# Retention and a two-layer MLP on one core: q loaded by the parity of the head, rows put in place by the stores

## The chip, the core and the metric

The kernel runs on one core of a Trainium2 chip. The metric is the device time of one launch in microseconds (us). The core has a matrix engine (TensorE, PE in the profile), VectorE (DVE), ScalarE (ACT), GpSimd (POOL) and SyncE (SP), and 16 DMA engines that move data between HBM and the on-chip memory. Transfers are issued from the queues of SP, ACT and POOL.

## The reference

Eight batches, eight heads, 576 positions, head size 64; then an MLP over the 4608 tokens with 512 inputs, 2048 hidden values and 512 outputs.

```python
scores = scale * np.matmul(q, k.transpose(0, 1, 3, 2))      # q, k, v: (8, 8, 576, 64), float32
Dmat = np.where(rel >= 0, gamma[:, None, None] ** rel[None, :, :], 0.0)   # rel = query - key
attn_out = np.matmul(scores * Dmat[None], v)                # (8, 8, 576, 64)
x = attn_out.transpose(0, 2, 1, 3).reshape(B * S, H * D)    # 4608 tokens x 512
h = x @ w_in
out = (h * np.cos(h)) @ w_out                               # 4608 x 512, float32
```

Each head has its own decay gamma. The decay by distance is split into a factor on q (growing with the position in a chunk) and one on v (falling), so that a chunk needs a mask of zeros and ones only, and a running state carries what lies before it.

## The kernel before, in words

**Chunks.** A batch is cut into five chunks r of up to 128 positions: four of 128 and one of 64. `ns_of(r)` is 2 or 1, the number of consecutive tokens that one partition holds of a chunk. Partitions 0 to 63 hold heads 0 to 3 and partitions 64 to 127 heads 4 to 7.

**Loads (`load`, lines 273 to 283).** q, k and v of a chunk are each loaded by two transfers on SP's queue, one for each half of the heads. A transfer runs over 64 partitions, 4 heads and one run of `ns` tokens of 64 floats: 256 runs of 512 B (256 B in the short chunk). The staging tiles kn, qn and vn exist once per chunk index r, so the load of the next batch waits for the casts of this one.

**Preparation (`prep_dma`, lines 326 to 336).** POOL casts k to bf16 (`kcast`), multiplies q and v by their decay factors (`decay`, line 317, with the tables UQ and WV), and one DMA transpose on SP (line 332) puts k and q with the head's 64 dimensions on partitions into KQT, which exists twice (batch even or odd). Then SP issues the loads of a chunk that lies three chunks further on. SP's queue is in order: transpose of one chunk, then six loads of a later one. Batches 0 and 1 are transposed on PE instead (`turn`, line 338, copied out by ACT in line 348).

**Attention.** `scores` (line 372) multiplies k and q of a chunk on PE into the two banks SC; DVE multiplies by the mask MK into RT (line 389). `rest` (line 394) adds the part from the running state (ps from kqt and sb), the part within the chunk (ps from rt and vb) and the new state. ACT copies the result into XT (line 439), the input of the MLP in bf16, 512 channels over 128 partitions by 4, with 1536 token columns used in a ring. That copy writes with a step of `ns`, which puts the columns into the order of the tokens. `state` (lines 444 to 459) updates the state with DVE and ACT.

**MLP.** A block j is 512 columns of XT. `mlp1` multiplies by w_in, ACT takes the cosine as a sine with an offset (line 482, tile cb) and DVE multiplies (line 485, tile gt or ss). `layer2` multiplies by w_out in seven products of half size in place of eight, with sums made by DVE; DVE totals (line 571) the result into OSB. `store` (line 490) writes 128 rows of 512 floats to HBM from ACT's queue in one transfer of 128 runs of 2 KB.

**Order of the work.** It is written out by hand in `emit` (lines 678 to 819). In the steady part, each block j runs 16 times `mlp1`, then `layer2(j)`, and between its products the five visits of batch j+1: `rest` of the chunk before and `scores` of the next one. The casts and transposes of later chunks (PREP1, PREP2) are placed in the same order. The stores of a block stand at the end of `layer2` (two, line 616) and after the fourth `mlp1` of the next block (two, line 804). The last block has an order of its own (`last_layer2`, line 621): three stores from ACT's queue (lines 647 to 650) and two from SP's (lines 660 and 662).

**Constants (`consts`, line 227).** POOL writes position numbers IP and MI with iota, DVE corrects them for the upper half of the partitions (line 243), and ACT makes UQ and WV with 16 Exp, one for each head and table (line 260).

Of the kernel before, what the change touches and what calls it, by code (L numbers as in the profile page):

```python
# [13 lines left out]
DM = H_ * D_  # L14
# [29 lines left out]
def ns_of(r):  # L44

    return ck_of(r) // 64


class Tok:
# [91 lines left out]
class _Kernel:  # L141
    def __init__(self, nc, es, q, k, v, w_in, w_out, out):
# [51 lines left out]
        self.OSB = sb("osb", [128, 4 * DM], F32)  # L194
        self.bOSB = [Buf() for _ in range(4)]
        self.IP = sb("ip", [128, NIP], F32)
        self.WV = sb("wv", [128, NIP * 4], F32)
        self.UQ = sb("uq", [128, NIP * 4], F32)
        self.MK = sb("mk", [128, 2 * CH], BF16)
# [6 lines left out]
        self.bIP, self.bWV, self.bUQ, self.bMK, self.bC, self.bID, self.bIDLE = (Buf() for _ in range(7))  # L206

        def ps(name):
            return nc.alloc_psum_tensor(name, [128, 512], F32)
# [17 lines left out]
    def consts(self):  # L227
        s = self.s
        s.op("dve", lambda e: e.memset(self.C_LN8.ap(), float(math.log(1.0 / 8.0))), writes=[Buf()])
        s.op("dve", lambda e: e.memset(self.C_PIH.ap(), float(math.pi / 2.0)), writes=[self.bC])  # L230
        s.op("dve", lambda e: e.memset(self.IDLE.ap(), 0.0), writes=[self.bIDLE])
        self.touch(AF.Exp)

        for t, b, o, n, pat, base, mul in (
                (self.IP, self.bIP, 0, NIP, [[CH, NCH - 1], [1, 2]], 0, 2),
                (self.IP, self.bIP, NIP - 1, NIP, [[0, 1]], CH * (NCH - 1), 1),
                (self.MI, self.bMK, 0, 2 * CH, [[-1, 2], [1, 2], [2, 64]], 0, -2)):
            shape = [[n, 128]] + [[1, 1]] if o else [[n, 128], [1, n - 1]] if n == NIP else [[n, 128], [128, 2], [64, 2], [1, 64]]
            s.op("pool", lambda e: e.iota(bass.AP(t, o, shape), pat, base=base, channel_multiplier=mul,
                                          allow_small_or_imprecise_dtypes=True), writes=[b])  # L240
        for o, n in ((0, NIP - 1), (NIP - 1, 1)):
            up = bass.AP(self.IP, 64 * NIP + o, [[NIP, 64], [1, n]])
            s.op("dve", lambda e: e.tensor_scalar(up, up, -128.0 if n > 1 else -64.0, None, ALU.add),
                 reads=[self.bIP], writes=[self.bIP])
# [12 lines left out]
        for t, b, sign in ((self.UQ, self.bUQ, 1.0), (self.WV, self.bWV, -1.0)):  # L257
            for h in range(H_):
                hs, hh = divmod(h, 4)
                s.op("act", lambda e: e.activation(  # L260
                    bass.AP(t, 64 * hs * 4 * NIP + hh, [[4 * NIP, 64], [4, NIP]]),
                    bass.AP(self.IP, 64 * hs * NIP, [[NIP, 64], [1, NIP]]), AF.Exp, scale=sign * self.lng[h],
                    **(dict(bias=bass.AP(self.C_LN8, 64 * hs, [[1, 64], [1, 1]])) if sign > 0 else {})),
                    reads=[self.bIP, self.bC], writes=[Buf()])
            b.w = [Tok("act", "act", s.count["act"], {})]

    def touch(self, f):

# [16 lines left out]
    def w_in_load(self, i, after=()):  # L285
        n = DFF // NWI
# [22 lines left out]
        self.s.op(eng, fn, reads=[self.bST32["k"][r]], writes=[self.bKB[i][r]])  # L309

    def decay(self, eng, x, b, r):
        ns, i = ns_of(r), b % 2
        if x == "q":
            o, bt, w, bw = self.by_head(self.KQ[i][r], 256 * ns, 512 * ns, ns, D_, 256), self.bQB[i][r], self.UQ, self.bUQ
        else:
            o, bt, w, bw = self.by_head(self.VB[i][r], 0, 256 * ns, ns, D_ * ns, D_), self.bVB[i][r], self.WV, self.bWV
        self.s.op(eng, lambda e: e.tensor_tensor(  # L317
            o, self.by_head(self.ST32[x][r], 0, 256 * ns, ns, D_ * ns, D_),
            bass.AP(w, r * 8, [[4 * NIP, 128], [1, 4], [4, ns], [0, D_]]), ALU.mult),
            reads=[self.bST32[x][r], bw], writes=[bt])  # L320

    def kqt(self, i, r, x, n):

# [48 lines left out]
    def scores(self, b, r):  # L372
        s, ns, i = self.s, ns_of(r), b % 2
        W, nq = 2 * NP * S_, 64 * ns
        mms = []
        for c in range(2):
            for sl in range(ns):
                for hs in range(2):
                    for hp in range(2):
                        k0 = 64 * hp * W + 1024 * r + c * 128 + 64 * hs  # L380
                        mms.append((
                            bass.AP(self.SC[hp], 64 * hs * 512 + (c * ns + sl) * nq, [[512, 64], [1, nq]]),
                            bass.AP(self.KQT[i], k0 + sl * 256, [[W, 64], [1, 64]]),
                            bass.AP(self.KQT[i], k0 + 256 * ns, [[W, 64], [256, ns], [1, 64]]),
                            dict(start=c == 0 and sl == 0, stop=c == 1 and sl == ns - 1, skip_group_check=True)))
        self.group(mms, [self.bKT[i][r], self.bQT[i][r]], self.bSC)
        for hp in range(2):
            p3 = [[512, 128], [ns * nq, 2], [1, ns * nq]]
            s.op("dve", lambda e: e.tensor_tensor(  # L389
                bass.AP(self.RT[r % 2][hp], 0, p3), bass.AP(self.SC[hp], 0, p3),  # L390
                bass.AP(self.MK, 0, [[2 * CH, 128], [0, 2], [1, ns * nq]]), ALU.mult),
                reads=[self.bSC[hp], self.bMK], writes=[self.bRT[r % 2][hp]])

    def rest(self, b, r, state=True):
# [3 lines left out]
        if r:  # L398
            sb = self.SB[(r - 1) % 2]
            mms += [(bass.AP(self.PS, 512 * hs + 256 * c, [[1024, 128], [1, nq]]),  # L400
                     bass.AP(sb, (2 * hs + c) * 128, [[512, 128], [1, 128]]),
                     bass.AP(self.KQT[i], 1024 * r + 256 * ns + c * 128 + 64 * hs, [[W, 128], [256, ns], [1, 64]]),
                     dict(start=c == 0, stop=False, skip_group_check=True)) for c in range(2) for hs in range(2)]
        for c in range(2):
            for sl in range(ns):
# [29 lines left out]
        for x0, po0, n in ((t0, 0, n0), (0, n0 // ns, ck - n0)):  # L435
            if n:
                o = bass.AP(self.XT, x0, [[NP * XR, 128], [XR, NP], [1, ns], [ns, n // ns]])
                p = bass.AP(self.PS, po0, [[1024, 128], [256, NP], [64, ns], [1, n // ns]])
                s.op("act", lambda e: e.activation(o, p, AF.Copy),  # L439
                     reads=[self.bPS], writes=self.bXT[x0 // GR:(x0 + n) // GR])  # L440
        if state:
# [45 lines left out]
            bass.AP(m, 0, [[512, 128], [n, k], [1, n]]), bass.AP(cb, 0, [[TB, 128], [n, k], [1, n]]), ALU.mult),  # L487
            reads=[bm, bcb], writes=[x for d in dts for x in self.g(j, d)[1]])

    def store(self, j, m, eng="act"):  # L490
        row0 = TB * j + 128 * m
        self.s.dma(eng, f"o{m}", lambda e: e.dma_start(
            bass.AP(self.out, row0 * DM, [[DM, 128], [1, DM]]),
            bass.AP(self.OSB, m * DM, [[4 * DM, 128], [1, DM]])), reads=[self.bOSB[m]])

    def half_store(self, j, m, h, eng, b):
        row0 = TB * j + 128 * m
        self.s.dma(eng, f"o{m}{h}", lambda e: e.dma_start(
            bass.AP(self.out, row0 * DM + 256 * h, [[DM, 128], [1, 256]]),
            bass.AP(self.OSB, m * DM + 256 * h, [[4 * DM, 128], [1, 256]])), reads=[b])  # L500

    def mlp2(self, j, st, part):

# [344 lines left out]
```

## Time and profile before

| what | value |
|---|---|
| median of 3 runs | 308.84 us (305.84 to 311.0) |
| the profiled execution | 309.18 us, its span 307.1 us |
| mean granted PE clock | 0.989 |
| packets of the DMA queues | 103480, 49.60 MB |
| period of one block in the steady part | 30.4 us (stores at 159.26 and 189.66) |
| median landing of a store, a q load, a transpose | 3.4, 3.4, 4.3 us after the issue |

The span runs from the first to the last instruction of the profiled execution. The page lists the busy time of each engine, the packets of each DMA queue with the share of 16 engines' time that they took, the chain of work that ended last, groups of equal instructions, and the DMA issues with the time from issue to landing. A share above 1 of the DMA engines means that the times of packets in flight overlap.

### The profile page before, as it was taken

How to read it: one execution, taken by the hardware profiler on the slowest of the kernel's cores; microseconds unless marked ns; L12 is line 12 of the kernel's file. 1: busy time of each engine (PE TensorE's matmuls, PEld its weight loads, DVE VectorE, ACT ScalarE, POOL GpSimd, SP SyncE). 2: the span in 40 equal slices, each digit the busy share in tenths (PEclk: the TensorE clock that was granted, in tenths of full speed). 3: DMA queues.
4: the chain of work that ended last, by engine and by line, in shares of the span. 5: the costliest groups of instructions: out<-in, count | busy, mean ns of one | idle time of the engine just before them, and what ended most of it. 6: DMA issues, size and time to landing. Idle time of an engine off the chain costs nothing.

```text
span 307.1 us, 8716 instructions
## 1 busy us (share of the span) xinstructions
PE 292.3 (95%) x3520; PEld 190.6 (62%) x3520; DVE 232.3 (76%) x393; ACT 190.1 (62%) x336; POOL 115.8 (38%) x133
## 2 busy tenths in 40 slices
PE   8768997999899999999999999999999999999996
PEld 3347644553587458746874687457845874685485
DVE  3347654867986898789878986999689768937963
ACT  6647845587565766576657665865576657724730
POOL 2346271999835444533551445436341000000000
PEclk9969999999999999999999999999999999999999
DMA  4999999567986987697879799977795012003003
GB/s 137 204 203 218 215 235 235 156 162 198 235 177 184 280 129 189 169 269 161 164 180 260 160 174 170 290 168 173 191 254 97 2 50 89 2 0 130 10 0 140
DMA packets 103480, 49.60 MB, mean 162 GB/s; under 512 B 45456, under 2 KB 98960, under 8 KB 103440
## 3 DMA queue, kind: packets, MB, share of 16 engines
q1 hardware_dynamic: 94176, 35.80, 54.2%
q10 hardware_dynamic: 5040, 9.05, 8.8%
q0 software_dynamic: 4224, 4.19, 8.4%
q8 instruction: 28, 0.46, 0.6%
q14 instruction: 12, 0.10, 0.1%
HBM read 36.70 MB, written 9.44 MB: 150 GB/s over the span
## 4 chain that ended last, share of the span: by engine, by line
PE 82%; DVE 5%; ACT 4%; SPq 4%; DMA 2%; issue 1%; POOL 0%; DVEq 0%; ACTq 0%
PE mm L362 59%; PE mm L364 14%; PE ps L362 6%; SPq L281 4%; PE sc L362 3%; DMA kn<-in_k_dram 2%; ACT cb L482 2%; DVE gt L485 1%; DVE ss L542 1%; DVE rt L389 1%; ACT sb L456 1%; ACT xt L439 1%; ACT kqt L348 1%; DVE ss L485 1%; DVE s L453 0%
## 5 line engine op out<-in xcount | busy, mean ns | idle before, releaser
L362 PE MATMUL mm<-xt,win 128*128 128x512 bf16 (+5 forms) x517 | 119.0, 349 | 2.0 <-DVE gt L485 1.2
L482 ACT ACTIVATE cb<-mm,c_pih 128x512 bf16<-128x512 f32 (+3 forms) x147 | 98.7, 680 | 33.7 <-PE mm L364 30.0
L485 DVE TENSOR_TENSOR gt<-mm,cb 128x512 bf16<-128x512 f32 (+1 forms) x130 | 85.7, 678 | 11.8 <-ACT cb L482 8.2
L362 PEld LDWEIGHTS mm<-xt,win 128*128 128x128 bf16 x517 | 46.8, 99 | 49.5 <-ACT cb L482 4.0
L364 PE MATMUL mm<-xt,win 128*128 128x512 bf16 (+5 forms) x147 | 54.0, 368 | 0.0
L389 DVE TENSOR_TENSOR rt<-sc,mk 128x512 bf16<-128x512 f32 (+1 forms) x80 | 44.8, 601 | 11.4 <-PE sc L364 11.4
L308 POOL CAST kq<-kn 128x512 bf16<-128x512 f32 (+1 forms) x40 | 25.2, 629 | 66.3 <-DMA kn<-in_k_dram 66.3
L317 POOL TENSOR_TENSOR kq<-qn,uq 128x512 bf16<-128x512 f32 (+1 forms) x37 | 36.9, 997 | 20.8 <-DMA qn<-in_q_dram 19.1
L362 PE MATMUL mm<-tt,ss 128*128 128x256 bf16 x336 | 43.2, 273 | 0.0
L439 ACT ACTIVATE xt<-ps 128x512 bf16<-128x512 f32 (+1 forms) x41 | 27.0, 661 | 24.6 <-PE ps L364 18.6
L317 POOL TENSOR_TENSOR vb<-vn,wv 128x512 bf16<-128x512 f32 (+1 forms) x34 | 34.4, 1013 | 17.1 <-DMA vn<-in_v_dram 14.4
L456 ACT ACTIVATE sb<-s 64x256 bf16<-64x256 f32 x64 | 26.6, 416 | 13.3 <-DVE s L453 12.1
L362 PEld LDWEIGHTS mm<-tt,ss 128*128 128x128 bf16 x336 | 31.4, 98 | 4.8
L566 ACT ACTIVATE sn<-mm 128x512 f32<-128x512 f32 x31 | 18.5, 598 | 25.1 <-PE mm L364 24.8
L542 DVE TENSOR_TENSOR ss<-gt 128x512 bf16<-128x512 bf16 (+1 forms) x56 | 32.1, 573 | 0.9
L571 DVE TENSOR_TENSOR osb<-mm,sn 128x512 f32<-128x512 f32 x30 | 20.6, 687 | 11.6 <-PE mm L364 11.3
L362 PE MATMUL mm<-wout,gt 128*128 128x256 bf16 x217 | 28.0, 273 | 0.3 <-DVE gt L485 0.3
L362 PE MATMUL mm<-wout,ss 128*128 128x256 bf16 (+1 forms) x160 | 27.4, 305 | 0.0
L453 DVE TENSOR_TENSOR s<-ps,s 128x256 f32<-128x256 f32 x24 | 10.2, 424 | 21.3 <-ACT xt L439 19.7
L364 PEld LDWEIGHTS mm<-xt,win 128*128 128x128 bf16 x147 | 14.4, 98 | 15.9
L362 PEld LDWEIGHTS mm<-wout,gt 128*128 128x128 bf16 x217 | 20.1, 98 | 4.1 <-DVE gt L485 0.5
L362 PEld LDWEIGHTS mm<-wout,ss 128*128 128x128 bf16 x160 | 15.1, 98 | 5.2
(76 smaller groups left out, 324.6 us busy)
## 6 DMA issues: line engine op xcount, KB each, us to landing
out_dram<-osb ACTq DMA_DIRECT2D x34, 256.0 KB, 3.4
kn<-in_k_dram SPq DMA_DIRECT2D x64, 128.0 KB, 3.4
qn<-in_q_dram SPq DMA_DIRECT2D x64, 128.0 KB, 3.4
vn<-in_v_dram SPq DMA_DIRECT2D x64, 128.0 KB, 3.7
win<-in_moe_w_in_dram POOLq DMA_DIRECT2D x4, 512.0 KB, 7.4
wout<-in_moe_w_out_dram POOLq DMA_DIRECT2D x4, 512.0 KB, 11.6
kn<-in_k_dram SPq DMA_DIRECT2D x16, 64.0 KB, 3.7
qn<-in_q_dram SPq DMA_DIRECT2D x16, 64.0 KB, 3.0
```

Of the source, the lines that this page charges most:

```text
L308: fn = (lambda e: e.activation(o, x, AF.Copy)) if eng == "act" else (lambda e: e.tensor_copy(o, x))
L317: self.s.op(eng, lambda e: e.tensor_tensor(o, self.by_head(self.ST32[x][r], 0, 256 * ns, ns, D_ * ns, D_), bass.AP(w, r * 8, [[4 * NIP, 12 ...
L362: self.nc.tensor.matmul(o, a, b, **kw)
L364: return s.done("pe", self.nc.tensor.matmul(o, a, b, **kw), reads, writes)
L389: s.op("dve", lambda e: e.tensor_tensor(bass.AP(self.RT[r % 2][hp], 0, p3), bass.AP(self.SC[hp], 0, p3), bass.AP(self.MK, 0, [[2 * CH, 128 ...
L439: s.op("act", lambda e: e.activation(o, p, AF.Copy), reads=[self.bPS], writes=self.bXT[x0 // GR:(x0 + n) // GR])
L456: s.op("act", lambda e: e.activation(bass.AP(self.SB[r % 2], 64 * hp * 512 + 64 * hp, [[512, 64], [128, NP], [1, D_]]), bass.AP(self.S32, ...
L482: s.op("act", lambda e: e.activation(ci, mi, AF.Sin, bias=self.C_PIH.ap(), scale=1.0), reads=[bm, self.bC], writes=[bcb])
L485: s.op("dve", lambda e: e.tensor_tensor(bass.AP(gt, dt * TB + o0, [[16 * TB, 128], [TB * step, k], [1, n]]), bass.AP(m, 0, [[512, 128], [n ...
L542: self.s.op(eng, lambda e: e.tensor_tensor(oo, xx, yy, op), reads=xb + yb, writes=ob)
L566: self.s.op("act", lambda e: e.activation(self.SN[k].ap(), bank[0].ap(), AF.Copy), reads=[bank[1]], writes=[self.bSN[k]])
L571: self.s.op("dve", lambda e: e.tensor_tensor(bass.AP(self.OSB, 2 * t * DM + 256 * h, [[4 * DM, 128], [DM, 2], [1, 256]]), bass.AP(bank[0], ...
```

## The change

- **q's load.** A chunk of q is still two transfers on SP's queue, but now one for each parity of the head. Four partition groups of 32 hold the four head pairs, and a partition holds four consecutive tokens (`nj_of`: 4, or 2 in the short chunk) of both heads of its pair. A transfer is 4 head pairs x 32 runs of 1 KB (512 B in the short chunk). k and v are loaded as before.
- **Constants.** q's factors need position numbers of their own (IQ) and, since each group of partitions has other heads, a table LG of the logarithms, written by 16 memsets. UQ takes two Exp over all partitions and WV four.
- **Scores.** The moving operand reads q's columns in runs of 32 in place of 64. The columns of a chunk are now in the queries' order of the new layout (j, then t, for token 4t + j); MI, and so the mask, follows it.
- **x.** The copy into XT no longer steps: x stays in that order, and so do the rows of the MLP's result.
- **Stores.** The token that a row belongs to is found by `rows`; a store writes 32 rows with a step of four (two) rows, once for each j. Where the 128 columns of a store lie in one chunk it is one transfer, else two of 64 rows. In two batches (nine stores) four lie in one chunk and five do not; all of the last block's do not.

```diff
     def load(self, x, b, r, after=()):
         ns = ns_of(r)
         t, bt = self.ST32[x][r], self.bST32[x][r]
+
+        def parity(h):
+            n = D_ * nj_of(r)
+            dst = bass.AP(t, h * n, [[2 * n, 128], [1, n]])
+            src = bass.AP(self.src[x], ((b * H_ + h) * S_ + CH * r) * D_, [[2 * S_ * D_, 4], [n, 32], [1, n]])
+            return lambda e: e.dma_start(dst, src)
...
-        return self.s.dma("sp", f"{x}n{r}", [half(0), half(1)], writes=[bt], after=after)
+        parts = [parity(0), parity(1)] if x == "q" else [half(0), half(1)]
+        return self.s.dma("sp", f"{x}n{r}", parts, writes=[bt], after=after)
...
+        for h in range(H_):
+            for o, n, hd in ((0, 32, 2), (2, 64, 4)):
+                p, i = h // hd, h % hd
+                s.op("dve", lambda e: e.memset(bass.AP(self.LG, n * p * 6 + o + i, [[6, n], [1, 1]]),
+                                               self.lng[h] if o == 0 else -self.lng[h]), writes=[Buf()])
...
+        for t, b, n, w, o, c in ((self.IQ, self.bIQ, 32, 2 * NIP, 0, 2 * NIP - 2), (self.IP, self.bIP, 64, NIP, 0, NIP - 1)):
+            for p in range(1, 128 // n):
+                for o, m, k in ((0, c, CH), (c, w - c, 64)):
+                    up = bass.AP(t, n * p * w + o, [[w, n], [1, m]])
+                    s.op("dve", lambda e: e.tensor_scalar(up, up, -float(k * p), None, ALU.add),
+                         reads=[b], writes=[Buf()])
...
+        for t, bt, ip, bi, o, n in ((self.UQ, self.bUQ, self.IQ, self.bIQ, 0, 2),
+                                    (self.WV, self.bWV, self.IP, self.bIP, 2, 4)):
+            for i in range(n):
...
         if x == "q":
-            o, bt, w, bw = self.by_head(self.KQ[i][r], 256 * ns, 512 * ns, ns, D_, 256), self.bQB[i][r], self.UQ, self.bUQ
+            o = bass.AP(self.KQ[i][r], 256 * ns, [[512 * ns, 128], [D_, 2], [128, nj], [1, D_]])
+            x = bass.AP(t, 0, [[256 * ns, 128], [D_ * nj, 2], [D_, nj], [1, D_]])
+            w, bw, bo = bass.AP(self.UQ, 8 * r, [[4 * NIP, 128], [1, 2], [2, nj], [0, D_]]), self.bUQ, self.bQB[i][r]
...
-                            bass.AP(self.KQT[i], k0 + 256 * ns, [[W, 64], [256, ns], [1, 64]]),
+                            bass.AP(self.KQT[i], 64 * hp * W + 1024 * r + 256 * ns + 32 * (2 * hs + c),
+                                    [[W, 64], [128, 2 * ns], [1, 32]]),
...
-                o = bass.AP(self.XT, x0, [[NP * XR, 128], [XR, NP], [1, ns], [ns, n // ns]])
-                p = bass.AP(self.PS, po0, [[1024, 128], [256, NP], [64, ns], [1, n // ns]])
+                o = bass.AP(self.XT, x0, [[NP * XR, 128], [XR, NP], [1, n]])
+                p = bass.AP(self.PS, po0, [[1024, 128], [256, NP], [1, n]])
...
-    def store(self, j, m, eng="act"):
-        row0 = TB * j + 128 * m
-        self.s.dma(eng, f"o{m}", lambda e: e.dma_start(
-            bass.AP(self.out, row0 * DM, [[DM, 128], [1, DM]]),
-            bass.AP(self.OSB, m * DM, [[4 * DM, 128], [1, DM]])), reads=[self.bOSB[m]])
+    def rows(self, c):
+
+
+        b, c = divmod(c, S_)
+        r, c = divmod(c, CH)
+        return b * S_ + CH * r + c // 32, nj_of(r)
+
+    def store(self, j, m, eng="act", h=None, b=None):
+
+        col, n = (0, DM) if h is None else (256 * h, 256)
+        (r0, s0), (r1, s1) = (self.rows(TB * j + 128 * m + 64 * i) for i in range(2))
+
+        def part(p0, row, k, step):
+            src = bass.AP(self.OSB, p0 * 4 * DM + m * DM + col, [[4 * DM, 32 * k], [1, n]])
+            dst = bass.AP(self.out, row * DM + col, [[DM, k], [step * DM, 32], [1, n]])
+            return lambda e: e.dma_start(dst, src)
+
+        fn = [part(0, r0, 4, s0)] if r1 == r0 + 2 and s0 == s1 else [part(0, r0, 2, s0), part(64, r1, 2, s1)]
+        self.s.dma(eng, f"o{m}" + ("" if h is None else str(h)), fn, reads=[b or self.bOSB[m]])
```

More of the change, by code (lines that the diff above doesn't have):

```diff
@@ L46, in ns_of, with nj_of @@
     return ck_of(r) // 64
+def nj_of(r):
+    return ck_of(r) // 32
 class Tok:
@@ L205, in __init__ @@
         self.C_PIH = sb("c_pih", [128, 1], F32)
-        self.bIP, self.bWV, self.bUQ, self.bMK, self.bC, self.bID, self.bIDLE = (Buf() for _ in range(7))
+        self.bIP, self.bIQ, self.bLG, self.bWV, self.bUQ = (Buf() for _ in range(5))
+        self.bMK, self.bC, self.bID, self.bIDLE = (Buf() for _ in range(4))
         def ps(name):
@@ L241, in consts @@
[L241 to L244, printed above, removed]
+        for t, b, o, dims, pat, base, mul in (
+                (self.IQ, self.bIQ, 0, [[2 * NIP, 128], [4, NCH - 1], [1, 4]], [[CH, NCH - 1], [1, 4]], 0, 4),
+                (self.IQ, self.bIQ, 2 * NIP - 2, [[2 * NIP, 128], [1, 2]], [[1, 2]], CH * (NCH - 1), 2),
+                (self.IP, self.bIP, 0, [[NIP, 128], [1, NIP - 1]], [[CH, NCH - 1], [1, 2]], 0, 2),
+                (self.IP, self.bIP, NIP - 1, [[NIP, 128], [1, 1]], [[0, 1]], CH * (NCH - 1), 1),
+                (self.MI, self.bMK, 0, [[2 * CH, 128], [128, 2], [32, 4], [1, 32]], [[-1, 2], [1, 4], [4, 32]], 0, -2)):
+            s.op("pool", lambda e: e.iota(bass.AP(t, o, dims), pat, base=base, channel_multiplier=mul,
+                                          allow_small_or_imprecise_dtypes=True), writes=[b])
@@ L256, in consts @@
             s.op("dve", lambda e: e.memset(self.SB[i].ap(), 0.0), writes=[self.bSB[i]])
-        for t, b, sign in ((self.UQ, self.bUQ, 1.0), (self.WV, self.bWV, -1.0)):
-            for h in range(H_):
-                hs, hh = divmod(h, 4)
+        for t, bt, ip, bi, o, n in ((self.UQ, self.bUQ, self.IQ, self.bIQ, 0, 2),
+                                    (self.WV, self.bWV, self.IP, self.bIP, 2, 4)):
+            for i in range(n):
                 s.op("act", lambda e: e.activation(
[L261 to L265, printed above, removed]
+                    bass.AP(t, i, [[4 * NIP, 128], [n, 4 * NIP // n]]), ip.ap(), AF.Exp,
+                    scale=bass.AP(self.LG, o + i, [[6, 128], [1, 1]]),
+                    **(dict(bias=self.C_LN8.ap()) if o == 0 else {})),
+                    reads=[bi, self.bLG, self.bC], writes=[Buf()])
+            bt.w = [Tok("act", "act", s.count["act"], {})]
     def touch(self, f):
@@ L311, in decay @@
     def decay(self, eng, x, b, r):
[L312 removed]
+        ns, nj, i = ns_of(r), nj_of(r), b % 2
+        t, bt = self.ST32[x][r], self.bST32[x][r]
         if x == "q":
[L314 to L320 removed]
+            o = bass.AP(self.KQ[i][r], 256 * ns, [[512 * ns, 128], [D_, 2], [128, nj], [1, D_]])
+            x = bass.AP(t, 0, [[256 * ns, 128], [D_ * nj, 2], [D_, nj], [1, D_]])
+            w, bw, bo = bass.AP(self.UQ, 8 * r, [[4 * NIP, 128], [1, 2], [2, nj], [0, D_]]), self.bUQ, self.bQB[i][r]
+        else:
+            o = self.by_head(self.VB[i][r], 0, 256 * ns, ns, D_ * ns, D_)
+            x = self.by_head(t, 0, 256 * ns, ns, D_ * ns, D_)
+            w, bw, bo = bass.AP(self.WV, 8 * r, [[4 * NIP, 128], [1, 4], [4, ns], [0, D_]]), self.bWV, self.bVB[i][r]
+        self.s.op(eng, lambda e: e.tensor_tensor(o, x, w, ALU.mult), reads=[bt, bw], writes=[bo])
     def kqt(self, i, r, x, n):
@@ L488, in mlp1 @@
             reads=[bm, bcb], writes=[x for d in dts for x in self.g(j, d)[1]])
-    def store(self, j, m, eng="act"):
-        row0 = TB * j + 128 * m
-        self.s.dma(eng, f"o{m}", lambda e: e.dma_start(
-            bass.AP(self.out, row0 * DM, [[DM, 128], [1, DM]]),
-            bass.AP(self.OSB, m * DM, [[4 * DM, 128], [1, DM]])), reads=[self.bOSB[m]])
+    def rows(self, c):
[11 more added lines that the diff above has]
+        self.s.dma(eng, f"o{m}" + ("" if h is None else str(h)), fn, reads=[b or self.bOSB[m]])
     def half_store(self, j, m, h, eng, b):
[L497 to L500, printed above, removed]
+        self.store(j, m, eng, h, b)
     def mlp2(self, j, st, part):
```

19 lines of the change are left out of this document (9 added, 10 removed).

## The prediction

> **What bounds the kernel now.** I read the busy table first, then the chain of work that ended last, then the lists of DMA queues and issues, then the windows by stage, and last single stretches of the timeline.
>
> ```profile
> span 307.1 us, 8716 instructions
> PE 292.3 (95%) x3520; PEld 190.6 (62%) x3520; DVE 232.3 (76%) x393; ACT 190.1 (62%) x336; POOL 115.8 (38%) x133
> ...
> q1 hardware_dynamic: 94176, 35.80, 54.2%
> q10 hardware_dynamic: 5040, 9.05, 8.8%
> q0 software_dynamic: 4224, 4.19, 8.4%
> ...
> PE 82%; DVE 5%; ACT 4%; SPq 4%; DMA 2%; issue 1%; POOL 0%; DVEq 0%; ACTq 0%
> ...
> out_dram<-osb ACTq DMA_DIRECT2D x34, 256.0 KB, 3.4
> ...
> qn<-in_q_dram SPq DMA_DIRECT2D x64, 128.0 KB, 3.4
> ```
>
> PE is busy for 95% of the span and holds 82% of the chain; SPq (4%) and DMA (2%) are the start alone. q1 is SP's queue (loads, transposes), q10 is ACT's (stores), q0 POOL's (weights). So shorter work elsewhere buys little, and the question is whether anything that PE waits for becomes late. The windows show what stands in reserve:
>
> ```profile
> core 0: us, PE busy (x) PEld busy (x) DVE busy (x) ACT busy (x) POOL busy (x), PEclk, DMA share, GB/s
> ...
> 159.30:189.70 30.40, 30.40 (x403) 20.60 (x401) 25.39 (x45) 20.25 (x36) 13.61 (x16) 1.00 1.02 197
> ...
> 251.50:277.50 26.00, 26.00 (x187) 17.14 (x185) 19.07 (x33) 14.50 (x23) 0.00 (x0) 1.00 0.11 41
> ```
>
> One period (a block of 512 tokens, one batch prepared) is 30.4 us, PE full throughout at granted clock 1.00. The DMA share is 1.02: packets of two queues are in flight at once, and the 16 DMA engines have little to give. Slack of the preparation: the last transposes and the use of what they make.
>
> ```profile
> 229.78 3.97 SPq L332 DMA_TRANSPOSE kqt<-kq  x3
> ...
> 249.97 0.23 PE L362 MATMUL sc<-kqt 64*64 64x64 bf16 x7
> ...
> 251.41 0.48 DVE L389 TENSOR_TENSOR rt<-sc,mk 128x128 bf16<-128x128 f32 x2
> ```
>
> The third transpose is issued at 232.5 and lands, by the shortest landing of that line (2.5 us), at 235.0; PE reads it at 250.0. So a transfer may be late by about 15 us here before PE stands.
>
> **Packet prices.** From the queue lists of windows in which one kind runs nearly alone:
>
> ```profile
> q1 hardware_dynamic: 2279, 1.10, 48.4%
> ...
> q1 hardware_dynamic: 3122, 0.77, 39.9%
> ...
> DMA  0000001999999700000000000009999997000000
> ...
> q10 hardware_dynamic: 576, 1.05, 34.9%
> ```
>
> Window 0 to 8 us, loads of 512 B: 48.4% of 16 engines times 8 us, over 2279, is 27.2 ns a packet on one engine. Window 230 to 240, transposes (250 B): 20.4 ns. Window 251 to 259, stores of 2 KB (512 of the 576): 87 ns; the DMA line of that window, the mean share of all 16 engines in slices of 0.2 us, stands at nine tenths and more during each pair of stores, so all 16 take part. A 1 KB packet, by the straight line from 27.2 to 87: 47 ns.
>
> **The change part by part.**
>
> *Start constants.* DVE gains 16 memsets at 0.06 us and eight tensor_scalars at 0.26, loses two: +2.5 us, where it stands idle 2.57 us before the first q lands. ACT drops from 16 Exp (2.8 us) to six; POOL gains two iotas of 0.19. Hidden; without that cover up to 2.5 us.
>
> *SP's issues.* A load of 256 packets holds SP 0.62 us, a transfer of 128 packets 0.34 (the half store on SP). Two q loads a chunk: 0.56 us less, 40 times, 22 us of SP's queue. On the path this counts only at the start, where the chain runs through SP until the k load of chunk 3: three chunks ahead of it, 1.7 us. Bounds 0 to -1.7, since that load then takes 7.09 us to land behind the weights.
>
> *Which engines carry q and the stores.* This decides. Before, both patterns of a load begin with 64 partitions, those of a store with 128 rows, and 16 engines share a transfer: 16 packets each of a half load, 8 of a store. The new q source begins with 4 head pairs, each of 32 rows of 1 KB; the new store's target begins with 4 (one chunk) or 2 (each of two parts). No row has a transfer with so small an outer count, so bounds: all 16 engines, or 4 and 2. The nearest rows by size say 16, but they fit a dealing by flat packet list and one by outer count equally. [...]
>
> On engine 0, per batch. k and v: eight full loads of two halves at 16 packets of 512 B, 256, and 64 of 256 B: 7.0 + 1.3 = 8.3 us. q: four full loads of two transfers at 32 packets of 1 KB, 256, and 64 of 512 B: 12.0 + 1.7 = 13.8 (was 4.1). Transposes: 4.5 times 1024 packets over 16, 288 at 20.4, 5.9. A whole store on four engines is 32 packets, 2.8 us; in two parts on two engines 64, 5.6 us (was 0.7). A batch is 4.5 blocks of 128 columns, so of nine stores in a row four stay whole and five straddle two chunks: 17.4 us per four. Sum 45.4 us against the period's 30.4 (before: 21.1). Engine 0 falls 15 us behind per period and eats the slack in one; k, v and transposes have a share on it too, so all land late. SP's queue fills, and the transposes queue behind the loads. What is late next: PE runs in order, so behind a score matmul that waits for its transpose stand the products of layer 2, and behind them ACT's sines and DVE's products; nothing else of PE can fill the gap.
>
> Sum up to the last transpose: loads 8 x 22.1 = 177; transposes 6 x 5.9 = 35; weights 256 x 47 ns = 12; stores of six blocks (12 whole, 12 split) 34 + 67 = 101. That is 325 us, begun at 2.2 (the first packets of window 0 to 8): landed at 327 instead of 235. PE then has what it had from 250.0 to 307.1: 57.1, so 384. Tail: the last five stores are all split, 3 x 5.6 + 2 x 3.0 (64 of 1 KB) = 22.8 us on engine 0, from 302.56 on plus the 1.35 us that a store takes beyond its packets, and 0.3 to the end: 327.0, i.e. 19.9 more. Span 404; the profiled execution lasted 309.18 for a span of 307.1, so 406. The median of the three runs, 308.84, is 0.3 below that one.
>
> *Parts on ACT and PE.* The copy xt now writes one run (748 ns before; 598 for the plain 128x512 copy sn): 150 ns x 31 less, of which its 1% of the chain keeps at most 0.6 us. Some 19 more issues on ACT: between nothing (0.17 each by packet count) and 0.34 each, 6.5 us, beside ACT's 30 us of waiting for PE; 0 taken. If ACT's queue fills, cb behind the store is late and gt after it. Score and ps matmuls read q in runs of 32 instead of 64: going from one run of 128 (219 ns, mm 128x128) to two of 64 (221) costs 2 ns, so four runs some 2 to 6 ns on 640, 1 to 4 us; 0 taken, since PE now waits. The q product on POOL keeps 512 elements in runs of 64: 0. The mask on DVE too.
>
> **The rivals.** *Few engines, but the two queues side by side* (an engine serves a load and a store at once). Loads and transposes are 28.0 us a period, stores 17.4, both under 30.4: no lag but the tail. ACT's three last stores are 14.2 us from 303.9 on, end 318.4: +11.3, 320.5 us. For it: a share above 1. Against: in window 128.9 to 159.3 the stores' packets take 11.9% of 16 x 30.4, 113 ns instead of 87; they wait for each other.
>
> *All 16 engines share them still* (the other side). Then q is 3.4 us per engine and batch (64 x 47 ns, 16 x 27.2) in place of 4.1, nothing is late, and only the start (-1.7 at best), xt (-0.6) and a second issue at the very end (+0.34) are left: 307 to 309.5, 308. It decides from 6.2 engines up: per period k, v and transposes are 14.2 us whatever the count, q and four stores 55 + 45 us shared by the count, and 14.2 + 100/6.2 is 30.4. For it: the stores of window 251 to 259 do keep all 16 busy. Against: their outer count was 128.
>
> **How the numbers follow.** Few engines taking turns 0.68, 406 us; its own range is 374 (10% of overlap) to 449 (stores at 113 ns, weights at the page's 98). Side by side 0.15, 320. All sixteen 0.17, 308. Range 316 to 450, which leaves out the last case and little else. A change under about 2% can't be told from none here. The last case splits into faster 0.04, same 0.12 and slower 0.01; the other two, 0.83, are slower, which makes 0.84.
>
> **What would show it.** Right: PE busy well under 95%, PE or PEld waiting for kqt's transposes; the mean DMA share falling (four engines full, twelve idle) while q and store landings grow past 5 us; SP's issues of 0.34 us stretched by full queues; a tail of some 20 us of DMA after the last DVE work. Wrong: q landing in 3 us as before and PE still at 95%. The step most in doubt is the count of engines, then whether loads and stores on one engine add up.

## The result and the profile after

The changed kernel takes 433.03 us (median of 4 runs, 430.48 to 434.32), the kernel before 308.15 us on the same chip (4 runs, 305.84 to 311.0): ratio 1.408, 95% interval 1.396 to 1.419. Forecast were 406 us and a range of 316 to 450. Ratios and intervals, here and below, are of the fast runs alone (those within 1.5% of the fastest of their kernel), medians of all runs. The profiled execution lasted 430.48 us, its span 428.6. The page of the kernel after, the lines that answer to those of before:

```profile
span 428.6 us, 8705 instructions
PE 315.0 (73%) x3520; PEld 198.4 (46%) x3520; DVE 231.0 (54%) x415; ACT 181.2 (42%) x326; POOL 114.3 (27%) x135
...
q1 hardware_dynamic: 82952, 35.80, 60.0%
q0 software_dynamic: 4224, 4.19, 6.1%
q10 hardware_dynamic: 4620, 9.04, 5.9%
...
PE 39%; DMA 27%; ACTq 11%; SPq 6%; ACT 5%; issue 3%; DVE 2%; POOL 1%; DVEq 0%; POOLq 0%
...
L391 PE MATMUL mm<-xt,win 128*128 128x512 bf16 (+5 forms) x517 | 126.8, 366 | 33.9 <-DVE gt L518 33.0
...
out_dram<-osb ACTq DMA_DIRECT2D x36, 128.0 KB
out_dram<-osb ACTq DMA_DIRECT2D x16, 256.0 KB
```

PE's share of the span falls from 95% to 73%, and in the chain from 82% to 39%; DMA (27%), ACT's issues (ACTq, 11%) and SP's (6%) take its place. The bytes are the same (queues q1, q10 and q0, in MB in the second column). The waits of the kernel after (columns: engine, line, what it waited for; us in total, times, longest) say for what:

```profile
DVE gt L518 <- ACT cb L515: 52.6, 52, 14.5
...
PE sc L391 <- DMA kqt<-kq: 37.4, 14, 12.7
PE mm L391 <- DVE gt L518: 33.0, 9, 13.8
ACT cb L515 <- issue: 31.4, 4, 15.0
```

There are two separate stalls. The scores wait 37.4 us for transposes (before, no such wait is listed); and `mm` from xt and win, the product of layer 1 on the page, waits 33.0 us for gt (DVE's product, which reads an earlier result before PE writes over it), gt for the sine cb on ACT, and cb for "issue", that is, for ACT's own queue. One of the four times, on ACT's timeline (columns: start, us, engine, line):

```profile
128.82 0.70 ACT L515 ACTIVATE cb<-mm,c_pih 128x512 bf16<-128x512 f32 x1
129.24 15.22 ACTq L538 DMA_DIRECT2D out_dram<-osb  x3
144.56 1.84 ACT L515 ACTIVATE cb<-mm,c_pih 128x512 bf16<-128x512 f32 x3 [15.04 <-issue]
```

Three store transfers hold ACT's queue for 15.22 us, and the next sine stands behind them. All 54 store issues on ACT take 73.1 us here, the longest 6.3; before, 35 took 15.3 us and the longest 1.1.

**Which engines carry a transfer.** Queue q10 counts 5040 packets before and 4620 after. The data are 35 x 128 = 4480 packets in both; the rest is 560 before, 35 transfers x 16, and 140 after, which is 16 x 4 + 38 x 2 (16 whole stores, 38 parts). So a transfer ends with one more packet on each engine that it uses (before, in the window 251 to 259 us where all 16 engines are at work, four stores count 64 packets under 512 B beside their 512 of data), and the new stores use four or two, as the prediction's sum has it. SP's queue, q1, tells the same of q: it counts 94176 - 82952 = 11224 packets less, of which 10240 are data (80 loads of 128 packets in place of 256), 960 are 80 x 12 closing packets, and 24 are those of the last stores (32 before, 8 after). The tail shows the same by its rate. The DMA list for the window 405.5 to 428.6 us of the kernel after, where only split stores are left:

```profile
DMA  0111110111111111111111111111111111111000
GB/s 25 43 43 32 50 53 18 35 35 53 50 50 50 53 53 50 50 50 57 50 50 50 50 57 50 48 50 51 50 48 50 48 48 48 48 48 50 23 20 0
```

One tenth of 16 engines and 50 GB/s: two engines of about 25 GB/s each (2 KB in 84 ns, the median of these packets, is 24.4). The parts come from ACT's queue (386 packets in this window) and from SP's (264), so both use the same two.

**Where the 121.5 us went.** The mask of chunk 4 of batches 2 and 7 cuts the span into three stages:

| kernel | start, to the mask of (2,4) | five periods, to (7,4) | one period | end | span |
|---|---|---|---|---|---|
| before | 97.6 | 153.8 | 30.8 | 55.7 | 307.1 |
| after | 122.9 | 221.2 | 44.2 | 84.5 | 428.6 |
| difference | 25.3 | 67.4 | 13.5 | 28.8 | 121.5 |

### The profile page after: what moved, and what is told of

Same layout as the page of the kernel before. It is cut to its first block, busy times and chain, and to the rows that moved or that the text cites. A ratio compares the mean times of both kernels' runs of the same rounds, so it can differ in the third digit from the quotient of the medians.

```text
span 428.6 us, 8705 instructions
## 1 busy us (share of the span) xinstructions
PE 315.0 (73%) x3520; PEld 198.4 (46%) x3520; DVE 231.0 (54%) x415; ACT 181.2 (42%) x326; POOL 114.3 (27%) x135
## 3 DMA queue, kind: packets, MB, share of 16 engines
q1 hardware_dynamic: 82952, 35.80, 60.0%
q0 software_dynamic: 4224, 4.19, 6.1%
q10 hardware_dynamic: 4620, 9.04, 5.9%
## 4 chain that ended last, share of the span: by engine, by line
PE 39%; DMA 27%; ACTq 11%; SPq 6%; ACT 5%; issue 3%; DVE 2%; POOL 1%; DVEq 0%; POOLq 0%
PE mm L391 28%; DMA kqt<-kq 21%; ACTq L538 11%; PE mm L393 6%; SPq L307 5%; DMA kn<-in_k_dram 4%; ACT cb L515 3%; PE sc L391 2%; PE ps L391 2%; DMA qn<-in_q_dram 2%; SPq L301 1%; DVE gt L518 1%; ACT sb L489 1%; POOL kq L349 0%; DVE s L486 0%
## 5 line engine op out<-in xcount | busy, mean ns | idle before, releaser
L391 PE MATMUL mm<-xt,win 128*128 128x512 bf16 (+5 forms) x517 | 126.8, 366 | 33.9 <-DVE gt L518 33.0
L515 ACT ACTIVATE cb<-mm,c_pih 128x512 bf16<-128x512 f32 (+3 forms) x147 | 95.7, 680 | 86.5 <-PE mm L393 53.4
L518 DVE TENSOR_TENSOR gt<-mm,cb 128x512 bf16<-128x512 f32 (+1 forms) x130 | 85.0, 679 | 56.2 <-ACT cb L515 52.6
L391 PEld LDWEIGHTS mm<-xt,win 128*128 128x128 bf16 x517 | 47.9, 102 | 88.5 <-DVE gt L518 40.2
L393 PE MATMUL mm<-xt,win 128*128 128x512 bf16 (+5 forms) x147 | 56.3, 383 | 0.0
L391 PE MATMUL mm<-tt,ss 128*128 128x256 bf16 x336 | 46.1, 284 | 0.0
L391 PE MATMUL sc<-kqt 64*64 64x128 bf16 (+1 forms) x536 | 16.1, 231 | 38.9 <-DMA kqt<-kq 37.4
L349 POOL TENSOR_TENSOR vb<-vn,wv 128x512 bf16<-128x512 f32 (+1 forms) x34 | 35.2, 1036 | 22.0 <-DMA vn<-in_v_dram 20.8
L472 ACT ACTIVATE xt<-ps 128x512 bf16<-128x512 f32 (+1 forms) x41 | 22.2, 544 | 31.6 <-PE ps L393 28.8
L391 PEld LDWEIGHTS mm<-tt,ss 128*128 128x128 bf16 x336 | 32.6, 101 | 6.1 <-issue 0.3
L391 PEld LDWEIGHTS sc<-kqt 64*64 64x64 bf16 x536 | 10.1, 114 | 44.5 <-DMA kqt<-kq 39.0
L391 PE MATMUL mm<-wout,gt 128*128 128x256 bf16 x217 | 30.5, 289 | 0.0
L391 PE MATMUL mm<-wout,ss 128*128 128x256 bf16 (+1 forms) x160 | 29.5, 320 | 0.0
L586 DVE TENSOR_TENSOR ss<-gt 128x512 bf16<-128x512 bf16 (+1 forms) x56 | 28.3, 506 | 0.9
```

The costliest lines, as they stand in the source:

```text
L349: self.s.op(eng, lambda e: e.tensor_tensor(o, x, w, ALU.mult), reads=[bt, bw], writes=[bo])
L391: self.nc.tensor.matmul(o, a, b, **kw)
L393: return s.done("pe", self.nc.tensor.matmul(o, a, b, **kw), reads, writes)
L472: s.op("act", lambda e: e.activation(o, p, AF.Copy), reads=[self.bPS], writes=self.bXT[x0 // GR:(x0 + n) // GR])
L515: s.op("act", lambda e: e.activation(ci, mi, AF.Sin, bias=self.C_PIH.ap(), scale=1.0), reads=[bm, self.bC], writes=[bcb])
L518: s.op("dve", lambda e: e.tensor_tensor(bass.AP(gt, dt * TB + o0, [[16 * TB, 128], [TB * step, k], [1, n]]), bass.AP(m, 0, [[512, 128], [n ...
```

## The experiments

Two theories. **Theory A**, the prediction's: engine 0 carries a share of everything, and the sum of the packets on it sets the pace (45.4 us a period). **Theory B**: the engine that issues a transfer stands still while few engines take its packets, so the price is paid on ACT, and by the transposes behind it. Layouts with all 16 engines then tell what else the change costs. All times are medians, against the kernel before on the same chip (308.55 to 309.12 us).

**The two halves apart.** The q load of the change with the stores of before; and the kernel before with the new stores alone.

```diff
  e1 (from after):   fn = [part(...)]  ->  one transfer of 128 rows
  e7 (from before):  store()           ->  the store() and rows() of the change
```

> The changed kernel, with the stores as before the change (one transfer of 128 adjacent rows, 16 engines), so that the output's rows stay in the queries' order and are not put in place; the q loads stay on four engines. Theory (packets pile up on the first engines): engine 0 has 8.3 + 13.8 + 5.9 + 2.8 = 30.8 us of packets a period against 30.4, so it just keeps up; the stalls of ACT in its stores and the tail go: 309 to 325 us. Rival (the 1 KB q loads and the runs of 32 cost, the stores do not): still above 390 us. Rival (more issues and scattered rows cost, not the engines): 305 to 312 us, the same side as the theory; the other runs tell those apart.

> The kernel before, with the changed kernel's stores alone (the same transfers to the same rows, on four or two engines); q, the order of x and all else as before, so the output's rows are not in place. Theory now: the stores by themselves set the pace of the steady part, by stalling ACT while it issues them and by holding up the transposes that share engines 0 and 1; the period of a block rises by 11 to 13 us as in the run with q by head pairs, the tail by 20: 390 to 415 us. Theory of the prediction (only the sum of packets on engine 0 counts): 12.4 + 5.9 + 17.4 = 35.7 us a period against 30.4, 5 us more in each of five periods and 20 for the tail: 345 to 365 us.

e1: 332.84 us, 1.077 [1.072, 1.082]. e7: 399.66 us, 1.296 [1.289, 1.303]. In spans +24.1 and +90.6, together 114.7 of the 121.5: the halves nearly add up, and the stores are three quarters. e1 comes out above its range, and not where it was expected: its period is 31.9 us (the sum on engine 0 gives 30.8), but its start is 18.0 us longer. There the weights' packets of 1 KB on POOL's queue share the engines; they take 98 ns each (8.4% of 16 x 307.1 us over 4224, on the page of before), where the prediction had 47. That this is the reason was not tried by itself. The page and the waits of e7:

```profile
PE 36%; DMA 22%; SPq 17%; ACTq 11%; ACT 4%; issue 2%; DVE 2%; DVEq 0%
...
ACT cb L487 <- issue: 30.3, 4, 11.3
...
PE sc L367 <- DMA kqt<-kq: 20.7, 9, 8.6
```

Both stalls come back with the stores alone. Its period is 40.9 us, while the packets on engine 0 sum to 35.7 (45.4 with 4.1 for q in place of 13.8): theory A is 5 us short.

**Only the last block, and a quarter of the bytes.** e6b gives the new stores to the last block alone, e8 writes 512 B of each row's 2 KB in e7.

```diff
+        if j < NTB - 1:                     # e6b
+            fn = [one transfer of 128 rows]
-        col, n = (0, DM) if h is None else (256 * h, 256)
+        col, n = (0, DM // 4) if h is None else (256 * h, 64)      # e8
```

> The kernel before, with the changed kernel's stores in the last block alone (five stores in ten parts on two engines; the rows of that block are not in place). Theory: 22.8 us of packets on engine 0 stand after the last computing, as the prediction's tail has it: 327 to 331 us. Rival (the tail is only a wait for things late before): 309 to 313 us.

> As the run before, but each store writes only the first quarter of its rows (runs of 512 B; the other three quarters of the output are not written): the same issues on the same engines, with 27 ns a packet in place of 84. Theory (time of the packets on engines 0 and 1): the packets of a period on engine 0 are 12.4 + 5.9 + 5.4 = 23.7 us and nothing backs up; left is the longer issue of seven pieces a period: 312 to 330 us. Rival (it is the number of pieces and how they are dealt, whatever their size): within 10 us of the run before.

e6b: 329.36 us, 1.066 [1.062, 1.070]. From the start of the last DVE operation to the end it takes 23.0 us in place of 2.5, the tail by itself. e8: 317.85 us, 1.030 [1.024, 1.035], period 31.7, and ACT's 54 issues take 33.0 us, the longest 1.2. The same number of transfers, the same scattered rows and the same two or four engines: what costs most is the time of the packets on those engines; the number and the scattering are left with at most 3%.

**q on two engines.** e1 with each q load in four transfers whose outer size is 2. SP's queue counts 82976 packets as in e1 (160 x 2 closing packets in place of 80 x 4), so each uses two engines.

```diff
-            src = bass.AP(..., [[2 * S_ * D_, 4], [n, 32], [1, n]])
+            src = bass.AP(..., [[2 * S_ * D_, 2], [n, 32], [1, n]])      # for g in range(2)
```

> The run with the changed kernel's q loads and the old stores, but q in four transfers a chunk whose sources begin with 2 (two engines) instead of two that begin with 4; rows of the output stay in the queries' order. Same bytes, same runs, the same number of issues as in the run by head pairs on 16 engines (327.0 us). Theory (loads pile up by the sum of packets on engine 0): 8.3 + 27.5 + 5.9 + 2.8 = 44.5 us a period instead of 30.8, and some 45 us more in the first three batches: 395 to 440 us. Rival (number of issues on SP): 325 to 340 us.

417.16 us (two runs), 1.350 [1.342, 1.357], period 41.3 where the sum on engine 0 gives 44.5. For loads, theory A holds to within 7%: 30.8 and 44.5 against 31.9 and 41.3.

**All 16 engines by more transfers.** A group of 32 partitions has an outer size of 32, and the closing packets then show all 16 engines: ACT's queue counts 6720 packets in e9 and in e3, 4480 of data and 140 x 16, and SP's queue 85192 in e2, 2240 more than in the kernel after (160 x 16 in place of 80 x 4). e2 loads q in four such transfers and keeps the new stores; e9 writes each store in four transfers in the kernel before; e3 does both; e10 does only q, with the old stores; e4 is e10 with a copy into XT that puts the columns in order (step of four).

```diff
+            dst = bass.AP(t, 32 * p * 2 * n, [[2 * n, 32], [n, 2], [1, n]])
+            src = bass.AP(..., [[n, 32], [S_ * D_, 2], [1, n]])                          # e2, e3, e4, e10
+        fn = [part(64 * i + 32 * a, r + a, 1, s) ... for a in range(2)]                   # e3, e9
+                o = bass.AP(self.XT, x0, [[NP * XR, 128], [XR, NP], [1, nj], [nj, n // nj]])   # e4
```

> The changed kernel, with each chunk of q loaded by four transfers, one for each head pair, whose two patterns both begin with 32 (16 engines); the same 1 KB runs into the same places. Stores stay split, on four or two engines. Theory: engine 0 has 8.3 + 3.4 + 5.9 + 17.4 = 35.0 us a period against 30.4, so it falls behind by 4.6 a period, less the slack of 15, and the tail of 20 us and ACT's waits in its stores stay: 345 to 375 us. Rival (scattered rows and more issues): no gain from the loads, 425 to 440 us.

> The kernel before, with each store in four transfers of 32 rows on 16 engines (146 issues instead of 37), rows as in the run before the last, so not in place. Theory: an issue holds ACT for 0.44 us whatever its size, 12 more a period are 5.3 us of ACT in bursts of eight, behind which the sines stand: 5 to 6 us a period and 3 at the end: 335 to 350 us. Rival (that run was slow by its q loads): 309 to 315 us.

> As the run before, and each store in four transfers of 32 rows, one for each j, whose patterns begin with 32 (16 engines): the same rows to the same places, with 4 issues for a store instead of 1 or 2 (146 in all instead of 58). Theory (engines): nothing piles up; issues of ACT cost some 0.5 us a store more, beside its waits: 305 to 318 us. Rival (issues and scattered rows): more than two and a half times the issues, so above 430 us. Rival (runs of 32 on PE, the new order of x): still far above 309, since both stay.

> q loaded by head pairs on 16 engines; the copy into XT steps by four columns and puts the tokens in order, as the kernel before the change did with a step of two; stores as before, one transfer each. Theory: no piling up and no further issue on ACT; PE is the bound again: 303 to 309 us, at best 2 us below the kernel before, by the start. Rival (runs of 32 on PE cost): 1 to 4 us above the kernel before.

> The changed kernel with q loaded by head pairs on 16 engines and the stores of before (rows of the output stay in the queries' order). The copy into XT does not step. Theory: four issues of 0.61 + 3 x 0.43 us stand in place of two of 0.62 on SP, 0.7 us a chunk; SP then needs 33 us for a batch and is the bound of the steady part instead of PE: 318 to 326 us, and the rest of the run with x in order (327.7 us) is the stepping copy. Rival (the stepping copy alone made that run slower): 305 to 310 us.

| kernel | us | ratio [95%] | period | sum of ACT's store issues, longest |
|---|---|---|---|---|
| e2 | 413.84 | 1.334 [1.324, 1.344] | 43.4 | 74.7, 6.1 |
| e9 | 353.69 | 1.149 [1.142, 1.157] | 37.0 | 75.6, 1.4 |
| e3 | 354.18 | 1.138 [1.128, 1.147] | 36.7 | 72.7, 1.5 |
| e4 | 327.72 | 1.058 [1.050, 1.065] | 33.5 | 14.3, 0.7 |
| e10 | 326.98 | 1.060 [1.055, 1.065] | 33.2 | 14.2, 0.7 |

All five come out above what was expected of them, e10 by 1 us only. e2 is the one that decides (its profiled execution lasted 417.04 us): with q on 16 engines, engine 0 has 35.0 us a period, and the period is 43.4. Its waits have both stalls still:

```profile
PE mm L391 <- DVE gt L518: 35.7, 11, 10.9
...
PE sc L391 <- DMA kqt<-kq: 30.0, 10, 9.3
```

So in the kernel after the sum on engine 0 (45.4 for a period of 44.2) is no full account; the stores alone would hold it nearly as long. e9 and e3 show that ACT's issues cost on 16 engines too: 140 issues at about 0.54 us. The page of e9, and one of its waits:

```profile
PE 53%; ACTq 16%; ACT 11%; DVE 8%; issue 5%; SPq 4%; DMA 2%; POOL 0%; DVEq 0%
...
out_dram<-osb ACTq DMA_DIRECT2D x136, 64.0 KB, 2.8
...
ACT cb L487 <- issue: 25.2, 7, 4.8
```

The stores land in 2.8 us and DMA holds 2% of the chain, but ACTq and ACT 27%. PE waits for a transpose only once there, 1.5 us, so this is the price of ACT's issues without late transposes. e10 points to the same on SP's queue. The four q transfers of a chunk take 2.2 us of it in place of 1.4 (100 to 220 us), and the scores wait again; the waits of e10:

```profile
PE sc L391 <- DMA kqt<-kq: 13.1, 7, 3.8
```

e4 against e10 gives the price of the stepping copy into XT: its mean grows from 544 to 1121 ns, and the median time by 0.7 us, which these runs can't tell from nothing (the two ratios lie in each other's intervals). e3 and e9 agree, so beside dear stores q by pairs costs nothing that shows.

**Stores from POOL's queue.** e7 with its stores issued by POOL, but for three of the last block (SP's two and the half store that names ACT), so that ACT is free of them until the end.

```diff
-    def store(self, j, m, eng="act", h=None, b=None):
+    def store(self, j, m, eng="pool", h=None, b=None):
```

> As the run with the changed kernel's stores alone on the kernel before (399.7 us), with all but the five or six issues of the last block that name their queue issued from POOL's queue instead of ACT's; rows not in place. ACT then never stands in an issue. Theory A (the packets that pile up on the first engines hold up the transposes, whoever issues): transposes still land in over 10 us at worst and the run stays above 350 us; what is gained is ACT's part, some 40 us. Theory B (what counts is ACT standing behind its full queue, the late transposes only follow): below 335 us. POOL's own issues, some 50 of 0.8 us, come on top of its 116 us of work in both.

371.61 us (median; 362.18 to 374.39, too far apart for an interval). Less than e7's 399.66, far above the 308.8 of before. Its page and its waits:

```profile
q0 software_dynamic: 18368, 13.20, 18.7%
...
POOL out_dram L510 <- DVE osb L587: 59.1, 7, 22.0
...
PE sc L367 <- DMA kqt<-kq: 35.2, 15, 8.0
```

With almost no store on ACT, cb no longer waits for issues, and the scores still wait 35.2 us for transposes. But POOL now stands 59.1 us waiting for osb, and the casts that feed the transposes stand behind it. Nor are the stores the same transfers: POOL's queue counts 18368 packets, 4224 of them the weights', so 14144 for 52 stores, where ACT's queue has 4620 for 54. From 308 to 313 us, where these stores alone are moving, they move 134 GB/s, which at 25 GB/s an engine takes more than five. So the run takes the stores off ACT and off the few engines at once. The time is on the side that was expected of theory A, but the run doesn't test it and splits nothing.

**q in two transfers on 16 engines.** The last kernel keeps the change's q load, two transfers of 128 runs of 1 KB, but puts token group t and head pair p on partition 4t + p. The outer sizes are then 128 and 32, and SP's queue counts 83936 packets, 960 more than in e1 (80 x 16 closing packets in place of 80 x 4): 16 engines. PE reads q's columns with a step of four; stores and the order of XT are those of before.

```diff
-            src = bass.AP(..., [[2 * S_ * D_, 4], [n, 32], [1, n]])
+            src = bass.AP(..., [[n, 32], [2 * S_ * D_, 4], [1, n]])
-   bass.AP(self.KQT[i], ... + 32 * (2 * hs + c), [[W, 64], [128, 2 * ns], [1, 32]])
+   bass.AP(self.KQT[i], ... + 2 * hs + c,        [[W, 64], [128, 2 * ns], [4, 32]])
```

> q in two transfers of 128 runs of 1 KB as in the changed kernel, but with the token group outermost (partition 4t + pair), so that the outer counts are 32 and 128 in place of 4; PE reads q's columns with a step of four, the copy into XT steps as in the kernel with q by pairs, and the stores are those of the kernel before. Theory (the outer count alone made the q load dear, and the four transfers of the kernel with q by pairs cost SP's queue, not the data): all 16 engines take part, SP issues two fewer long pieces a chunk, the period is 30.4 to 31.0 us, PE bound, and the time 305 to 311 us, ratio 0.99 to 1.01. Rival 1 (the layout of q itself costs, on POOL or in the copy into XT): as the kernel with q by pairs, 324 to 330 us. Rival 2 (a step of four in PE's moving reads halves their rate): 20 matmuls of 128 columns a chunk take 0.05 us longer each, 1.07 us x 36 chunks, 345 us.

325.51 us, 1.052 [1.048, 1.056]; period 32.6. The theory misses: the outer count was not all of the price. Rival 1 has the time, but not the cause; the page of this kernel:

```profile
PE 310.2 (96%) x3520; PEld 197.7 (61%) x3520; DVE 230.7 (71%) x418; ACT 206.6 (64%) x326; POOL 116.4 (36%) x136
...
PE 86%; ACT 4%; DVE 3%; SPq 3%; DMA 2%; issue 1%; POOL 0%; DVEq 0%
```

PE is full at 96% and no score waits for a transpose; the last one lands 30 us before its mask (16 before the change). PE has more to do, and PE's groups by shape show where. Before:

```profile
L362 PE MATMUL sc<-kqt 64*64 64x128 bf16 x480 | 13.0, 221 | 1.2 <-ACT kqt L348 1.2
L362 PE MATMUL ps<-kqt,sb 128*128 128x128 bf16 x96 | 9.4, 220 | 2.1 <-ACT sb L456 1.4 <-DVE rt L389 0.6
```

and in this kernel (busy us, mean ns of one):

```profile
L426 PE MATMUL sc<-kqt 64*64 64x128 bf16 x480 | 20.2, 288 | 2.2 <-ACT kqt L412 2.2
L426 PE MATMUL ps<-kqt,sb 128*128 128x128 bf16 x96 | 15.0, 290 | 2.2 <-DVE rt L456 1.8 <-DVE vb L384 0.3
```

The matmuls that read q with a step of four elements take 67 to 73 ns more for 128 columns; those that read rt without a step are as before (225). The busy time of these two groups and their four smaller ones grows by 7.2 + 5.6 + 2.3 + 1.0 + 0.4 + 0.4 = 16.9 us, which is the difference of the spans, 324.0 - 307.1 (PE's busy time as a whole grows by 17.9, its idle time falls by 1.0). That is rival 2 in kind, at less than half its size: it counted the score matmuls one after the other, while those on quarters of the array overlap (480 of 221 ns are 13.0 us of busy time).

## Why the prediction came out right, and which steps were wrong

The forecast of a large loss through few DMA engines was right; the time was 6% low. Of the two mechanisms that the runs show, it had one, the packets on few engines, and put the other, ACT standing in its issues, at nothing. That the period came out to 3% is in part luck.

- **Four and two engines: right.** No trace of the kernel before shows a count below 16, so the four and the two in the forecast's sum were the author's estimate. The closing packets (140 on ACT's queue, 960 fewer for q on SP's) and the 50 GB/s of the tail show them. Both rivals fall: 16 engines by the same count, side by side because the transposes do land late, up to 18.8 us after their issue (6.0 before).
- **Packets on engine 0 add up: right for loads, incomplete for stores.** That q's four engines and a store's two or four have one in common is an estimate too: the traces do not say which engine took a packet, and only the tail shows two queues on the same two. The period of 45.4 against 44.2 looks like proof and isn't, since e2 (35.0 against 43.4) and e7 (35.7 against 40.9) break the sum.
- **"0 taken" for more issues on ACT: the mis-sized term.** The prediction gave 19 more issues at most 6.5 us and left it at "if ACT's queue fills, cb behind the store is late". cb is late: ACT's issues take 73.1 us in place of 15.3, and even the shortest of them 0.52. How much of a store's price is ACT's and how much is the late transposes' stays open. e11 was to split it and changes both. e9 shows 41.3 us of span for 140 issues with hardly a wait for transposes, but those are other issues than these 54.
- **Transposes landing at 327: 336.0 measured.** Nine us late. The weights' packets at 98 ns in place of 47 would alone be 256 x 51 ns = 13 us, if they hold an engine that long; which term makes up for it was not tried.
- **PE's remaining 57.1 us.** From the landing to the first of the last stores the prediction had 302.56 - 250.0 = 52.6 us; it took 403.25 - 336.0 = 67.2. PE had three chunks to catch up, and is 6.7 us later at the last mask; then ACT stands in six issues for 9.0 us between 344.8 and 355.4 (one sine alone waits 6.28 us for two of them), and from that mask to the first of the last stores it is 8.0 more. This is the largest part of the 24.6 us by which the span exceeds the forecast (9.0 + 14.7 + 0.9).
- **Tail: right.** 24.45 us forecast from the first of the last stores to the end, 25.35 measured.
- **22 us of SP's queue saved: wrong.** The 0.34 us came from a store. A q load of 128 packets on 16 engines takes SP 0.61 us (e12), as one of 256 did. On four engines the 80 q issues take 73.8 us in all, against 60.3 before, since SP's issues stretch. From SP's timeline of the kernel after:

```profile
222.92 4.81 SPq L307 DMA_DIRECT2D vn<-in_v_dram  x2
227.83 8.65 SPq L361 DMA_TRANSPOSE kqt<-kq  x1
```

- **Small terms.** The copy xt fell from 661 to 544 ns in the mean. Runs of 32 on PE: the score matmuls take 224 ns in place of 221 in e10. Both were taken as nothing, rightly.
- **The signs.** PE well under 95%, waits for kqt, stretched issues and the tail all showed. That the DMA share would fall did not: it stands at 0.99 in 159 to 203 us, most likely since the time of a packet includes its waiting behind others: SP's packets of 256 B take 62.9 ns in the mean, 25.7 before, with a median of 18 in both. Only the tail, with one kind of transfer, shows the two engines. The landings of q loads and stores could not show, as the page of the kernel after gives none for them.

No version here beat the kernel before. Each way to a q load of long runs costs 5% or more: few engines (e1, 7.7%), more issues (e10, 6.0%), a step in PE's reads (e12, 5.2%).

## What to carry to other kernels

Before a transfer's patterns are changed, read their two outermost sizes: for the loads and stores from SP's and ACT's queues here, the number of DMA engines was 16 where both were 32 or more, and the smaller size where that was 4 or 2. The packets of one of them, times their price, were nearly the time where nothing else was on them (22.8 us by that sum in a tail of 25.35). Price a transfer on the queue that issues it as well, even when its landing is hidden: ACT spent 73.1 us in 54 issues here, and its sines stood 31.4 us behind them. And look for the full engine among those that read a new layout first: in e12 PE, at 96%, paid 16.9 us for it.

## What the runs showed of the hardware

**PE's granted clock behind one wait.** The windows of the kernel after, behind a wait of PE of 4.25 us that ends at 226.46:

```profile
core 0: us, PE busy (x) PEld busy (x) DVE busy (x) ACT busy (x) POOL busy (x), PEclk, DMA share, GB/s
...
226.40:231.50 5.10, 5.04 (x12) 1.79 (x13) 3.87 (x9) 2.32 (x4) 0.61 (x1) 0.50 2.41 145
232.40:235.90 3.50, 3.50 (x18) 1.61 (x17) 2.96 (x5) 2.65 (x5) 0.00 (x0) 1.00 0.13 51
```

PE is full in both, but at granted clock 0.50 in the first, for 5.1 us, with 12 matmuls where the second has 18 in 3.5 us (all 128x512, 631 to 634 ns in the mean in place of 379). So this wait cost more than its length. Over the whole span the mean granted clock is 0.890 in place of 0.989, and PE's busy time grows from 292.3 to 315.0 us for the same number of matmuls, most of it in products that the change leaves as they are (mm 128x512 takes 400 ns in place of 379).

**What an issue costs.** On 16 engines ACT takes 0.32 to 0.45 us (shortest to median) for transfers of 32 packets (e9) and 0.34 to 0.38 for 128 (before), so the number hardly counts, and SP a median of 0.61 for loads of 128 (e12) and 0.62 for 256 (before); on two or four engines ACT takes 0.52 to 0.57 (after, shortest to median). In the kernel after, one issue takes up to 6.34 us on ACT, and up to 9.27 for a transpose on SP.
